# Top-k attention and two gated layers on one core: weights converted in place, differences one step behind

## The chip, the core and the metric

The kernel runs on one core of a Trainium2 chip. The time is the device time of one execution in microseconds (us); for the kernel before it is the median of three runs. The engines are named TensorE (PE in the rows, with its weight loads as PEld), VectorE (DVE), ScalarE (ACT), GpSimd (POOL) and SyncE (SP, which only issues DMAs here; SPq is its queue of them).

## The reference

Attention over 4 batches, 8 heads, 576 positions and a head size of 64, in which each query keeps its 32 largest scores; then two layers on 2304 tokens, each a product with a weight of 512 x 2048, a function of each element, and a product with a weight of 2048 x 512.

```python
scores = scale * np.matmul(q, k.transpose(0, 1, 3, 2))
kth = np.partition(scores, -top_k, axis=-1)[..., -top_k:-top_k + 1]
scores = np.where(scores >= kth, scores, -1e9)
attn = softmax(scores)
x = np.matmul(attn, v)                      # to (2304, 512)

h = x @ w_in                                # layer 1
P = a[0] + a[1] * h + a[2] * h**2 + a[3] * h**3
Q = 1.0 + abs(b[0]) * abs(h) + abs(b[1]) * h**2
x = (P / (Q + 1e-06)) @ w_out

h = x @ w_in2                               # layer 2
out = (h * cos(h)) @ w_out2
```

The four weights come as 64-bit floats. The chip has none, so the kernel takes each as two 32-bit words and makes of it a 32-bit float `a`, a rounded high part `h` (type fp32r, which TensorE takes in one pass) and a low part `a - h`. A product is then the sum of three: high by high, high by low and low by high.

## The kernel before

The work is cut into 72 units of attention (a query tile of 128 rows and a pair of heads). A unit consists of scores (`qk`, TensorE into `sx`, copied by ScalarE to `sS`), the selection of the 32 largest (`topk`: MAX8 and MATCH_REPLACE8 on VectorE over `e`, with two TENSOR_TENSOR ahead and, behind ScalarE's exponential, two SCALAR_TENSOR_TENSOR), and the product with v (`av`: transposes `pp`, copies `pt`). Layer 1 runs 9 units behind (`in1` to `out1`) and layer 2 18 units behind (`in2` to `out2`), in blocks of 256 tokens and 256 columns (`g`). Each unit is cut into five pieces, and the code is written in the order of pieces; a planner with its own estimate of time then lays each engine's instructions in order, up to a window of pieces. From unit 20 on (`U0`) the order is written out by hand (`unit`).

The conversions are 64 steps of 128 x 512 weights, `conv(kind, c, x)` at line 264: kind 0 is layer 1's input weight and kind 1 its output weight, in turns of four (`convs`, line 693), 32 in all; kinds 2 and 3 are those of layer 2, 16 and then 16. A conversion loads a raw tile of 128 x 512 x 2 words on SP, 512 KB (line 274). ScalarE turns the high word into a float in a buffer `cb` of its own (line 277) and the low word in place (line 278). Then VectorE shifts `cb` by three bits (TENSOR_SCALAR, line 281), GpSimd adds the low word (line 282), and ScalarE makes `h`. For kinds 0, 2 and 3 (`CPE`) the low part is taken by TensorE, which adds `a` by the identity and `h` by its negative into PSUM (`diff`), and a copy by ScalarE; for kind 1 GpSimd subtracts (line 299). SP stores the low part in HBM (`w1lo`, `w1ol`, `w2lo`, and `w2o`, which takes both parts of kind 3), and the layers stream it in later, through `lo`, `w1ol` and `w2o` (lines 490 to 498). High parts of kinds 0 to 2 stay on chip.

For layer 1's weights there are 5 raw tiles and 6 buffers `cb` (`RA`, `CA`), for layer 2's 3 and 4 (`RB`, `CB`), in a pool that is closed and opened again between them, since `w2hi` takes the place (line 268). At most three conversions are under way (`CD`), and none of layer 2 starts before layer 1's are through (`pull`, line 735). How far conversions have to be is tied to the pieces: the first 36 by piece 46, all by piece 80 (lines 972 to 975), and by what a product needs (`need`).

## Time and profile before

| | |
|---|---|
| Median of three runs | 1339.47 us (1338.54 to 1341.24) |
| The profiled execution | 1339.15 us, span 1337.4 us |
| Busy share of the span | TensorE 92%, VectorE 86%, ScalarE 82%, GpSimd 43% |
| Granted TensorE clock, mean | 0.971 |
| First and last load of a raw tile | 6.3 and 289.4 us |
| DMA | 314.98 MB, 236 GB/s |

Times in the rows are microseconds from the span's start, and ns where marked. Busy shares of the whole are means over stages that are limited by different engines, so the rows below are cut by stage: conversions of layer 1's weights (to 140 us), of layer 2's (to 310 us), and the stretch without conversions.

### The profile page before, as it was taken

What the parts mean: (1) busy time and instruction counts of PE and PEld (TensorE: products, weight loads), DVE (VectorE), ACT (ScalarE), POOL (GpSimd) and SP (SyncE); (2) the same over time, 40 slices, a digit from 0 to 9 for tenths busy, and PEclk for the clock granted to TensorE, in tenths of its full rate; (3) what the DMA queues carried; (4) which work ended last, traced back from release to release, by engine and by line L of the source; (5) the groups of instructions that cost most, each with busy time, mean ns of one, the idle gap of its engine ahead of it and who ended that gap; (6) DMA issues with size and microseconds to landing.
All of it is one profiled execution on the core that took longest, in us unless ns stands there. A gap on an engine that the chain in (4) does not pass through costs nothing.

```text
span 1337.4 us, 25132 instructions
## 1 busy us (share of the span) xinstructions
PE 1233.8 (92%) x8992; PEld 1086.7 (81%) x8992; DVE 1156.0 (86%) x2498; ACT 1093.7 (82%) x1871; POOL 569.6 (43%) x469
## 2 busy tenths in 40 slices
PE   6675678888999999999999999999999999999998
PEld 3343455656889999999989899999999999999996
DVE  6999879979799999999999999999999998755633
ACT  7887788886888898888898888888898888877753
POOL 2656444453245555445554444454444444430000
PEclk9676999999999999999999999999999999999999
DMA  8986777884356777667677776666677778877774
GB/s 254 335 278 223 247 239 246 275 311 132 122 190 217 231 245 248 215 218 229 208 234 239 246 230 210 213 217 200 217 234 265 268 283 288 297 235 235 235 258 155
DMA packets 155948, 314.98 MB, mean 236 GB/s; under 512 B 12592, under 2 KB 47536, under 8 KB 155824
## 3 DMA queue, kind: packets, MB, share of 16 engines
q1 hardware_dynamic: 122832, 261.99, 59.3%
q10 hardware_dynamic: 32992, 51.39, 12.0%
q8 instruction: 71, 1.16, 0.4%
q14 instruction: 53, 0.43, 0.1%
HBM read 278.20 MB, written 35.13 MB: 234 GB/s over the span
## 4 chain that ended last, share of the span: by engine, by line
PE 62%; DVE 13%; ACT 12%; DMA 4%; issue 4%; POOL 3%; ACTq 1%; SPq 0%; POOLq 0%; DVEq 0%
PE h L80 24%; PE o L80 12%; PE sx L80 10%; PE y L80 10%; DVE e L80 6%; DVE hd L80 3%; ACT r L80 2%; DVE u L80 2%; DMA raw<-w 1%; ACT sS L80 1%; ACT e L80 1%; ACT cb L80 1%; PE diff L80 1%; DVE cb L80 1%; ACT u L80 1%
## 5 line engine op out<-in xcount | busy, mean ns | idle before, releaser
L80 DVE MAX8 hd<-e 128x8 f32<-128x288 f32 (+1 forms) x576 | 320.9, 595 | 0.0
L80 POOL TENSOR_TENSOR gg<-rr,gg 128x512 fp32r<-128x512 f32 x56 | 72.3, 1292 | 400.8 <-DVE rr L80 185.4
L80 DVE MATCH_REPLACE8 e<-hd,e 128x288 f32<-128x288 f32 (+1 forms) x432 | 230.7, 539 | 0.0
L80 PE MATMUL o<-w2o,gg 128*128 128x512 f32 x864 | 223.6, 398 | 0.0
L80 PE MATMUL y<-gg,w1o 128*128 128x256 f32 x1152 | 216.1, 286 | 7.0 <-ACT gg L80 4.5
L80 PEld LDWEIGHTS y<-gg,w1o 128*128 128x128 f32 x1152 | 182.6, 193 | 12.5 <-ACT gg L80 7.1
L80 PEld LDWEIGHTS o<-w2o,gg 128*128 128x128 f32 x864 | 153.8, 189 | 27.0 <-DVE gg L80 0.3
L80 PE MATMUL h<-xh,w1hi 128*128 128x256 f32 x576 | 171.1, 297 | 4.7 <-ACT xh L80 3.2
L80 PE MATMUL h<-xl,w1hi 128*128 128x256 f32 x576 | 164.2, 285 | 2.5 <-DVE xl L80 2.5
L80 PE MATMUL y<-gg,w1ol 128*128 128x256 f32 x576 | 164.0, 285 | 0.0
L80 PE MATMUL h<-x2l,w2hi 128*128 128x256 f32 x576 | 163.0, 283 | 0.0
L80 PE MATMUL h<-xh,lo 128*128 128x256 f32 x576 | 162.8, 283 | 0.0
L80 PE MATMUL h<-x2h,lo 128*128 128x256 f32 x576 | 162.7, 283 | 0.0
L80 PE MATMUL h<-x2h,w2hi 128*128 128x256 f32 x576 | 162.7, 283 | 0.0
L80 DVE TENSOR_TENSOR e<-sS 128x576 f32<-128x576 f32 x144 | 118.2, 860 | 39.6 <-POOL q L80 27.9
L80 POOL TENSOR_TENSOR cb<-cb,raw 128x512 int32<-128x512 int32 x64 | 88.2, 1383 | 99.7 <-DVE cb L80 75.3
L80 DVE SCALAR_TENSOR_TENSOR e<-sS,hd,e 128x576 f32<-128x576 f32 x144 | 123.0, 882 | 5.9 <-ACT e L80 4.4
L80 PEld LDWEIGHTS h<-xh,w1hi 128*128 128x128 f32 x576 | 109.6, 190 | 17.2 <-issue 5.9
L80 PEld LDWEIGHTS h<-xl,w1hi 128*128 128x128 f32 x576 | 109.9, 191 | 7.7 <-DVE xl L80 4.4
L80 PEld LDWEIGHTS y<-gg,w1ol 128*128 128x128 f32 x576 | 111.4, 193 | 0.7 <-issue 0.4
L80 ACT ACTIVATE e<-sS,nb 128x576 f32<-128x576 f32 x144 | 105.6, 771 | 7.7 <-DVE hd L80 6.0
L80 PEld LDWEIGHTS h<-x2l,w2hi 128*128 128x128 f32 x576 | 110.2, 191 | 0.5 <-issue 0.2
(1026 smaller groups left out, 3272.5 us busy)
## 6 DMA issues: line engine op xcount, KB each, us to landing
w2o<-w2o SPq DMA_DIRECT2D x144, 512.0 KB, 4.2
lo<-w1lo SPq DMA_DIRECT2D x72, 512.0 KB, 3.9
w1ol<-w1ol SPq DMA_DIRECT2D x72, 512.0 KB, 4.8
lo<-w2lo SPq DMA_DIRECT2D x72, 512.0 KB, 4.6
k<-kdr ACTq DMA_DIRECT2D x44, 576.0 KB, 5.6
raw<-w SPq DMA_DIRECT2D x32, 512.0 KB, 5.7
v<-vt ACTq DMA_DIRECT2D x48, 320.0 KB, 4.2
qr<-qt ACTq DMA_DIRECT2D x72, 128.0 KB, 2.7
```

Source lines behind the costliest of these rows:

```text
L80: r = f(*a, **k)
```

## The change

- A conversion has no buffer `cb` any more. The float, the shift, the sum and `h`'s source lie in the raw tile, in every second word; the low part is then written over the tile's first half as a dense row.
- There are two pools of raw tiles, `near` (left) and `far` (right), of six tiles each. Layer 1's conversions take them in turn, layer 2's only `far`, and `w2hi` takes the place of `near`, as four tiles that wait for the old ones tile by tile. The wait for layer 1's conversions to be through is gone.
- A conversion has three steps: load and first two operations; shift, sum and `h`; difference and store. `step` puts the difference of conversion m - 1 behind the loads up to m + 5 (m + 4 for layer 2) and ahead of the shift of m.
- The difference goes over TensorE and ScalarE for all kinds.
- `w1lo`, `w2lo` and `w1ol` lie in HBM by pairs of column tiles, so a store has rows of 1 KB for 512 B, and a load rows of 4 KB for 2 KB.
- Kind 3's `h` takes the buffers of the attention's `q` tiles, which are unused before unit 22.

```diff
-RA, CA, RB, CB = 5, 6, 3, 4
+RL, RR = 6, 6
-CD = 3
+CD = 4
-CPE = (0, 2, 3)
...
+        near, far = temp("near", "left"), temp("far", "right")
...
         def conv(kind, c, x):
...
-            raw = tmps[0].tmp.tile([P, CW, 2], I32, tag="raw", bufs=n1, name="raw" + nm)
-            SP.dma_start(out=raw, in_=src)
-            a = tmps[0].tmp.tile([P, CW], F32, tag="cb", bufs=n2, name="cb" + nm)
-            lo, hi, ai = raw[:, :, 0], raw[:, :, 1], a.bitcast(I32)
-            A.activation(a, hi.bitcast(F32), AF.Prelu, scale=2.0 ** -112, alpha=-2.0 ** 32)
+            at, n = (near, RL) if i < n_w1 and i % 2 else (far, RR)
+            raw = at.tmp.tile([P, CW, 2], I32, tag="raw", bufs=n, name="raw" + nm)
+            SP.dma_start(out=raw, in_=wd.rearrange("(c p) (f t) -> c p f t", p=P, t=2)[c, :, x * CW:(x + 1) * CW, :])
+            lo, ai = raw[:, :, 0], raw[:, :, 1]
+            a = ai.bitcast(F32)
+            d = raw.rearrange("p f t -> p (f t)")[:, :CW].bitcast(F32)
+            A.activation(a, a, AF.Prelu, scale=2.0 ** -112, alpha=-2.0 ** 32)
             A.activation(lo, lo.bitcast(U32), AF.Copy, scale=2.0 ** -29)
+            yield
...
+            V.tensor_scalar(ai, ai, 3, 0, op0=ALU.logical_shift_left, op1=ALU.bitwise_or)
+            G.tensor_add(ai, ai, lo)
...
+            A.activation(h, a, AF.Copy)
+            yield
...
-                else:
-                    G.tensor_sub(a, a, h.bitcast(F32))
+            PE.matmul(o, ident, a, start=True, stop=False)
+            PE.matmul(o, nident, h, start=False, stop=True)
+            A.activation(d, o, AF.Copy)
...
+        def step(s, n):
+            while state[s] < n:
+                m = state[s]
+                if s == 0:
+                    state["cq"].append(conv(*convs[m]))
+                else:
+                    step(0, min(m + 1 + (CD if m < n_w1 else RR - 3), len(convs)))
+                    step(s - 1 if s == 2 else 2, m + 1 if s == 2 else m)
+                next(state["cq"][m], None)
+                state[s] += 1
```

Where this moves instructions is shown at three places. In these rows a conversion's tiles bear its c and x and a running number; `raw_0_0_290<-w` is kind 0 or 2, `<-w1o` kind 1, `<-w2o` kind 3, and `cb` is the buffer that is gone.

GpSimd, in the first conversions, before:

```order
L80 TENSOR_TENSOR cb_3_0_318<-cb_3_0_318,raw_3_0_316 128x512
L80 TENSOR_TENSOR cb_0_0_334<-cb_0_0_334,raw_0_0_332 128x512
L80 TENSOR_TENSOR cb_1_0_348<-cb_1_0_348,raw_1_0_346 128x512
L80 TENSOR_TENSOR cb_0_0_334<-cb_0_0_334,w1o 128x512
L80 TENSOR_TENSOR cb_2_0_365<-cb_2_0_365,raw_2_0_363 128x512
L80 TENSOR_TENSOR cb_1_0_348<-cb_1_0_348,w1o 128x512
```

And after:

```order
L79 TENSOR_TENSOR raw_3_0_302<-raw_3_0_302 128x512
L79 TENSOR_TENSOR raw_0_0_306<-raw_0_0_306 128x512
L79 TENSOR_TENSOR raw_1_0_319<-raw_1_0_319 128x512
L79 TENSOR_TENSOR raw_2_0_335<-raw_2_0_335 128x512
L79 TENSOR_TENSOR raw_3_0_348<-raw_3_0_348 128x512
```

The sums follow each other; the subtractions (`<-cb,w1o`) are gone from this engine.

TensorE, in units 0 to 2, before:

```order
L80 MATMUL diff<-cb_3_0_318,ident 128x512
L80 MATMUL diff<-w1hi,nident 128x512
L80 MATMUL sx<-kraw_1_146,qr_160 128x288 x4
L80 MATMUL pp1a<-ident,e_181 128x128 x4
L80 MATMUL pp1b<-ident,e_181 128x128 x4
```

And after:

```order
L79 MATMUL pp1a<-ident,e_184 128x128 x4
L79 MATMUL diff<-raw_3_0_302,ident 128x512
L79 MATMUL diff<-w1hi,nident 128x512
L79 MATMUL pp1b<-ident,e_184 128x128 x4
L79 MATMUL sx<-kraw_1_149,qr_163 128x288 x2
L79 MATMUL diff<-raw_0_0_306,ident 128x512
L79 MATMUL diff<-w1o,nident 128x512
```

The differences stand later among the transposes and scores, and those of kind 1 (`<-w1o,nident`) have come to them.

SP's queue, where layer 2's first differences are stored, before:

```order
L274 DMA raw_0_1_1131<-w 128x1024
L274 DMA raw_1_1_1195<-w 128x1024
L307 DMA w2lo<-cb_0_0_1090 128x4x128
L274 DMA raw_2_1_1258<-w 128x1024
L175 DMA kdr<-kraw_3_1156 64x576 x4
L307 DMA w2lo<-cb_1_0_1095 128x4x128
L274 DMA raw_3_1_1274<-w 128x1024
```

And somewhat later in the same stage, after:

```order
L309 DMA w2lo<-raw_0_1_1112 128x2x256
L273 DMA raw_2_2_1299<-w 128x1024
L309 DMA w2lo<-raw_1_1_1130 128x2x256
L273 DMA raw_3_2_1409<-w 128x1024
L487 DMA lo_0_4_1580<-w1lo 128x1024
L309 DMA w2lo<-raw_2_1_1193 128x2x256
L273 DMA raw_0_3_1430<-w 128x1024
```

Before, a load reuses a raw tile that GpSimd has read. After, `raw_2_2` reuses the tile of `raw_0_1`, which the store one row ahead of it reads, and so on: each load waits for the landing of the store of the sixth conversion before it.

## Rows read from the trace of the kernel before

**Rows 1.** Busy time by stretch: TensorE, weight loads, VectorE, ScalarE, GpSimd; clock, DMA share, GB/s.
```profile
20.00:140.00 120.00, 83.82 (x340) 49.14 (x339) 118.85 (x253) 95.51 (x185) 73.85 (x54) 0.77 0.84 272
140.00:300.00 160.00, 124.94 (x734) 92.85 (x734) 132.78 (x273) 134.23 (x256) 76.90 (x56) 0.96 0.81 267
345.00:1000.00 655.00, 645.73 (x5064) 595.94 (x5063) 615.04 (x1390) 576.19 (x971) 314.04 (x270) 1.00 0.68 219
```

**Rows 2.** First transposes of units 0, 8, 16: ns min/median/max, first and last start.
```profile
L80 PE MATMUL pp0a<-ident,e x4: 415/421/421, 29.1 to 29.7; 128*128 128x128 f32 x4
...
L80 PE MATMUL pp8a<-ident,e x4: 272/273/299, 137.3 to 137.6; 128*128 128x128 f32 x4
...
L80 PE MATMUL pp16a<-ident,e x4: 421/421/447, 300.4 to 301.0; 128*128 128x128 f32 x4
```

**Rows 3.** Waits of VectorE, 140 to 300 us: total us, times, longest.
```profile
DVE cb L80 <- ACT cb L80: 13.2, 6, 6.5
DVE u L80 <- POOL u L80: 6.5, 2, 4.3
```

**Rows 4.** VectorE's groups, 20 to 140 us: busy us, mean ns, idle before.
```profile
L80 DVE MAX8 hd<-e 128x8 f32<-128x576 f32 x33 | 23.6, 743 | 0.0
L80 DVE TENSOR_SCALAR cb<-cb 128x512 int32<-128x512 int32 x30 | 22.2, 746 | 0.0
L80 DVE SCALAR_TENSOR_TENSOR e<-sS,hd,e 128x576 f32<-128x576 f32 x18 | 20.2, 1125 | 0.2 <-ACT e L80 0.2
L80 DVE TENSOR_TENSOR e<-sS 128x576 f32<-128x576 f32 x18 | 19.2, 1100 | 1.1 <-PE sx L80 0.8 <-ACT sS L80 0.2
L80 DVE MAX8 hd<-e 128x8 f32<-128x288 f32 x34 | 14.0, 443 | 0.0
```

**Rows 5.** The same view, 320 to 400 us.
```profile
L80 DVE SCALAR_TENSOR_TENSOR e<-sS,hd,e 128x576 f32<-128x576 f32 x10 | 7.8, 812 | 1.7 <-ACT e L80 1.6
...
L80 DVE TENSOR_TENSOR e<-sS 128x576 f32<-128x576 f32 x10 | 7.1, 749 | 3.1 <-POOL q L80 3.1
```

**Rows 6.** The shift in the same view, 0 to 20 and 140 to 300 us.
```profile
L80 DVE TENSOR_SCALAR cb<-cb 128x512 int32<-128x512 int32 x2 | 0.8, 412 | 0.0
...
L80 DVE TENSOR_SCALAR cb<-cb 128x512 int32<-128x512 int32 x31 | 14.7, 477 | 13.2 <-ACT cb L80 13.2
```

**Rows 7.** GpSimd's subtractions, 20 to 140 us.
```profile
L80 POOL TENSOR_TENSOR cb<-cb,w1o 128x512 f32<-128x512 f32 x16 | 21.8, 1363 | 3.2 <-ACT w1o L80 3.2
```

**Rows 8.** ScalarE's groups of the conversions, 20 to 140 us.
```profile
L80 ACT ACTIVATE raw<-raw 128x512 int32<-128x512 uint32 x28 | 18.9, 674 | 2.6 <-DMA raw<-w1o 1.6 <-DMA raw<-w 1.0
...
L80 ACT ACTIVATE w1o<-cb 128x512 fp32r<-128x512 f32 x16 | 10.0, 627 | 1.1 <-POOL cb L80 1.1
...
L80 ACT ACTIVATE cb<-diff 128x512 f32<-128x512 f32 x16 | 9.4, 589 | 1.1 <-PE diff L80 0.9
```

**Rows 9.** The chain that ended last, 140 to 300 us, by engine and line.
```profile
by line: issue 12.5%; DVE e L80 10.4%; POOL cb L80 6.9%; DMA raw<-w 6.7%; DMA raw<-w2o 6.6%; DMA w2lo<-cb 6.5%; ACT cb L80 5.2%; DVE hd L80 3.5%; POOL q L80 3.1%; PE h L80 3.1%; PE diff L80 3.0%; ACT u L80 2.7%; ACT raw L80 2.6%; PE sx L80 
```

**Rows 10.** TensorE's timeline: one difference at full clock; start, us.
```profile
65.42 1.10 PE L80 MATMUL diff<-cb,ident 128*128 128x512 f32 x2 [1.46 <-ACT cb L80]
65.96 0.79 PE L80 MATMUL diff<-w1hi,nident 128*128 128x512 f32 x1
```

**Rows 11.** Stores of layer 2's differences, 140 to 300 us: KB, median us to landing.
```profile
w2lo<-cb SPq DMA_DIRECT2D x16, 256.0 KB, 3.9
...
w2o<-cb SPq DMA_DIRECT2D x13, 256.0 KB, 5.5
```

**Rows 12.** SP's timeline: layer 2's first load, first store, last load, last store.
```profile
138.07 1.28 SPq L274 DMA_DIRECT2D raw<-w  x3
...
155.37 0.38 SPq L307 DMA_DIRECT2D w2lo<-cb  x1
...
289.44 0.33 SPq L274 DMA_DIRECT2D raw<-w2o  x1
...
307.73 0.32 SPq L302 DMA_DIRECT2D w2o<-cb  x1
```

More of the change, by code (lines that the diff above doesn't have):

```diff
@@ L161, in load_k0 @@
         def load_k0(pr):
-            x = tmps[0].tmp.tile([P, 2, S], F32R, tag="kraw", bufs=RQ, name=f"kraw0_{pr}")
+            x = near.tmp.tile([P, 2, S], F32R, tag="kraw", bufs=RQ, name=f"kraw0_{pr}")
             SP.dma_start(out=x[:, 0].bitcast(F32), in_=kt[0, pr])
@@ L254, in body @@
         b0, b1 = babs[:, 0:1], babs[:, 1:2]
-        whi = [wts.tile([P, NCC, DF], F32R, name="w1hi")]
-        wlo = [dr.tile([NF, P, NCC, P], F32, name="w1lo"), dr.tile([NF, P, NCC, P], F32, name="w2lo")]
+        w1hi = wts.tile([P, NCC, DF], F32R, name="w1hi")
+        whi = [[w1hi[:, c] for c in range(NCC)]]
+        wlo = [dr.tile([NG, P, NCC, BT], F32, name="w1lo"), dr.tile([NG, P, NCC, BT], F32, name="w2lo")]
         w1o = wts.tile([P, NF, DM], F32R)
-        w1ol = dr.tile([NF, P, DM], F32)
+        w1ol = dr.tile([NG, P, 2, DM], F32)
@@ L260, in body @@
         w2o = dr.tile([NF, P, 2, DM], F32)
         late, diff = [], {}
+        convs = []
+        for x in range(4):
+            convs += [(0, c, x) for c in range(NCC)] + [(1, 4 * x + c, 0) for c in range(4)]
+        n_w1 = len(convs)
+        convs += [(2, c, x) for x in range(4) for c in range(NCC)] + [(3, c, 0) for c in range(NF)]
         def conv(kind, c, x):
             nm = f"{kind}_{c}_{x}"
-            wd = (w1_d, w1o_d, w2_d, w2o_d)[kind]
-            src = wd.bitcast(I32).rearrange("(c p) (f t) -> c p f t", p=P, t=2)[c, :, x * CW:(x + 1) * CW, :]
@@ new lines, in conv @@
+            A.activation(a, a, AF.Prelu, scale=2.0 ** -112, alpha=-2.0 ** 32)
+            A.activation(lo, lo.bitcast(U32), AF.Copy, scale=2.0 ** -29)
+            yield
+            if kind == 2 and len(whi) == 1:
+                near.close()
+                wts2 = pool("wts2", reuse_waits="tile")
+                whi.append([wts2.tile([P, DF], F32R, name=f"w2hi{j}") for j in range(NCC)])
+            V.tensor_scalar(ai, ai, 3, 0, op0=ALU.logical_shift_left, op1=ALU.bitwise_or)
+            G.tensor_add(ai, ai, lo)
@@ new lines, in conv @@
+            if kind == 3:
+                h = att.tile([P, 2, 2, P], F32R, tag="q", bufs=QB, name="ch" + nm).rearrange("p a b t -> p (a b t)")
+            elif kind == 1:
+                h = w1o[:, c, :]
+            else:
+                h = whi[kind // 2][c][:, x * CW:(x + 1) * CW]
+            A.activation(h, a, AF.Copy)
+            yield
+            if "d" not in diff:
+                diff["d"] = ps_o.tile([P, 2, 512], F32, tag="o", name="diff")
+            diff["n"] = n = diff.get("n", 0) + 1
@@ L691, in store @@
                 (SP if c == 0 else A).dma_start(out=out[row:row + n, :], in_=ob[c * n:(c + 1) * n, :])
-        convs = []
-        for x in range(4):
-            convs += [(0, c, x) for c in range(4)] + [(1, 4 * x + c, 0) for c in range(4)]
-        n_w1 = len(convs)
-        convs += [(2, c, x) for x in range(4) for c in range(4)] + [(3, c, 0) for c in range(NF)]
         need = {}
@@ L723, in body, with pull @@
                 loads.append((need.get(e, 0), load_w2o, e[1], e[2]))
-        state = {"conv": 0, "cq": [], "load": 0, "nl": 0}
-        def cstart():
-            if state["conv"] < len(convs):
-                state["cq"].append(conv(*convs[state["conv"]]))
-                state["conv"] += 1
-        def cfinish():
-            state["cq"].pop(0)()
-        def pull(n):
-            while state["conv"] - len(state["cq"]) < n:
-                while len(state["cq"]) < CD and state["conv"] < len(convs) and (state["conv"] != n_w1 or not state["cq"]):
-                    cstart()
-                cfinish()
+        state = {0: 0, 1: 0, 2: 0, "cq": [], "load": 0, "nl": 0}
+        def step(s, n):
[3 more added lines that the diff above has]
+                    state["cq"].append(conv(*convs[m]))
+                else:
+                    step(0, min(m + 1 + (CD if m < n_w1 else RR - 3), len(convs)))
+                    step(s - 1 if s == 2 else 2, m + 1 if s == 2 else m)
+                next(state["cq"][m], None)
+                state[s] += 1
+        def pull(n, last=2):
+            step(last, n)
         def run_event(e):
@@ L750, in run_event @@
             if e[0] is out1 and e[2] == NG - 1 and not late:
-                tmps.pop().close()
-                late.append(pool("late"))
+                far.close()
+                late.append(pool("late", side="right", reuse_waits="tile"))
             e[0](*e[1:])
```

65 lines of the change are left out of this document (21 added, 44 removed).

## The prediction

> **What bounds the kernel now.** I read the busy times by stretch first, because the change touches only work that lies in the first 310 us. From 345 to 1000 us TensorE is busy 645.73 of 655 us [rows 1]: nothing that the change does can shorten that stretch, and whatever the stretches before it gain or lose arrives at the end one to one. So the question is how fast units 0 to 19 run. I split them at 140 us, where the conversions of layer 1's weights end and those of layer 2's begin.
>
> From 20 to 140 us VectorE is busy 118.85 of 120 us [rows 1], so it stands idle for 1.15 us: it is the bound, at 108.2 us for eight units (29.1 to 137.3, [rows 2]). But its own work is not what fills the time. In this stretch the operations that read two tensors take 1100 and 1125 ns, and the shift on the weights 746 ns [rows 4]; where GpSimd has little to do the same forms take 749 and 812 [rows 5], and the shift takes 412 [rows 6]. The forms with one input at the slow rate (MAX8) take 743 ns in the busy stretch, so it is not VectorE that is slow: the others wait for a port that GpSimd holds. The excess is 18 x 0.351 + 18 x 0.313 + 30 x 0.334 = 6.3 + 5.6 + 10.0 = 21.9 us.
>
> From 140 to 300 us no engine is full: VectorE 132.78, ScalarE 134.23, TensorE 124.94 of 160 [rows 1], and the eight units take 163.1 us (137.3 to 300.4). VectorE's 27 us of idle time are led by 13.2 us for the shift's input (ScalarE's first step of a conversion) and 6.5 us for layer 1's product [rows 3]. The chain that ended last shows why those are late: loads of raw tiles hold 6.7 and 6.6% of it there and stores of layer 2's differences 6.5% [rows 9], 19.8% of 160, or 31.7 us. Raw tiles are loaded only when one of three is free, and a conversion starts only when one of four result buffers has been stored.
>
> **The change, part by part.**
>
> *Layer 1's output weights on TensorE.* GpSimd loses 16 subtractions of 1363 ns, 21.8 us [rows 7], all of them in the first stretch, out of its 73.85 us there: 29.5%. VectorE waits for GpSimd in proportion to the time that GpSimd holds the port, so I take 29.5% of 21.9 us: -6.5 us, and since VectorE is the bound there, all of it on the path. Bounds: nothing, if only the additions behind each shift collide, and -10 us, if the subtractions, which followed at once, made the queues of two.
> ScalarE gains 16 copies of 589 ns, 9.4 us [rows 8]. It goes from 95.5 to some 106 of 113.5 us, 94%: hidden, but barely; without that cover at worst the 9.4 us come back. TensorE gains 16 differences. One takes 1.33 us from the first start to the last end at full clock (65.42 to 66.75, [rows 10]), so 21 us; its 83.82 us hold stretches at the low clock (mean 0.77 of full, [rows 1]), so there is room, and I take nothing, at worst a few us of later qk and transposes.
>
> *In place.* The same instructions now step over 8 bytes. On ScalarE a rounding copy of dense data takes 627 ns and a copy that reads and writes at that step 674 [rows 8]: 64 x 0.047 = 3 us over the whole stage, hidden beside work that isn't full. On GpSimd one operand was strided already; no cost taken. On VectorE no strided shift is in the trace. It could stay at 412, or fall to the slow rate: MAX8 gives (743 - 443) / 288 = 1.04 ns an element, so 443 + 224 x 1.04 = 677 ns for 512. The first is nearer, since the shift alone runs at well under the slow rate and keeps dtype and size; and the loss would be small: MAX8 doesn't wait for GpSimd, so 677 would stand against 746 in the first stretch (-2 us), and against 477 for 31 shifts in the second (+6 us, [rows 6]). I take 0 and keep +4 for the range.
> The Trainium skill, "VectorE: DVE Perf Modes", section on mode 2x_2P, asks of the fast mode for 32-bit data only that source and destination lie in SBUF and that their outermost dimension be even, not that the step be one. By it the term is 0, by the other end +4; no run here shows a strided shift yet.
>
> *Twelve raw tiles, then six, and the difference one step behind.* In the first stretch VectorE waits for nothing, so loads that come sooner gain nothing there. At the change of layer the old pools had to drain; now loads for layer 2 stand among the last stores of layer 1. In the second stretch a raw tile is held from its load to the landing of its difference: six tiles do what three raw and four result buffers did. The loads run four conversions ahead instead of two. I count against this what the new order puts on SP: a load of conversion m + 6 stands one to three rows behind the store of m and waits for its landing, and everything on SP, layer 1's streamed weights too, is queued behind it. A cycle of SP is then landing plus issues: 3.9 us for layer 2's input weights, 5.5 for its output weights [rows 11], each with 0.4 us for every DMA in between. Without overlap 16 x 5.0 + 10 x 6.9 = 149 us for the 26 loads that wait, 5.7 each. But two pairs of stores stand together before their two loads, and others have another store or a stream between, so I take off some 13 us: 136 us, 5.2 each. Before, 32 conversions took 138.1 to 307.7 us, 5.3 each.
> From the first store of layer 2 (155.4 before [rows 12]; I take 146, as its loads no longer wait for the drain) the last load then goes out at 146 + 136 = 282 us, where it was 289.4: 7 us sooner. From the other side: the two waits that a late raw tile explains are 13.2 us and the longest of the 6.5 us, 4.3: 17.5 us, and half of it would be 9. The two meet, and I take **-9 us**; bounds -20 (all such waits and half of the rest) and +5 (5.7 us a cycle: the last load at 294).
>
> *The rest.* Layer 2's input weights in four tiles, the wider rows of the two low parts in HBM, the pools that wait by tile: the same transfers and matmuls, under TensorE at 99% after 345 us. DMA engines are 68% busy there [rows 1]. Nothing.
>
> **The sum**: -6.5 + 0 - 9 = -15.5 us, rounded to -15. The span of 1337.4 becomes 1322.4; 1.75 us lie around it in the profiled execution (1339.15), which makes 1324.2, and the median stood 0.3 above that execution: **1324.5 us**.
>
> **The rivals.**
> *ScalarE takes VectorE's place* in the first stretch (94% by the sum, in order, with waits of its own): the -6.5 are lost and only the second stretch gains: 1331. For it: the margin; against: VectorE's work is far ahead in its queue, and it was idle for 1.15 us.
> *The stalls go altogether*: VectorE keeps only its waits for scores and half of the rest, -20, and -9 in the first stretch: 1310. Against: every load of the second half waits for a landing.
> *Slower: SP's queue is the new bound.* At 5.7 us a cycle the last load leaves at 294, 5 us late, and a difference that is one step behind adds a cycle, 5.7, before the last store: +10.7, less 6.5: 1343.5. It decides from 5.3 us a cycle on, the pace before; the landings of [rows 11] lie on both sides of that. Against it: landings were measured with loads in the queue ahead of them, and a queue that waits has fewer of these. The Trainium skill, "DMA: Bandwidth & Descriptors", section on the anatomy of one DMA, says that semaphore waits are held by the issuing sequencer before dispatch; this rival is that rule at work on SP.
> *The change doesn't do what it says*: the planner lays the loads as late as before, or the shift falls to the slow rate and the copies crowd ScalarE. Gains and losses cancel: within 3 us of 1339.
>
> **How the numbers follow.** Forecast (1316 to 1330) 0.52; ScalarE as bound, or another half gain (1330 to 1336) 0.15; stalls gone (below 1316) 0.11; cancelled (within 0.2%, 2.7 us, about what a measurement can tell from no change) 0.09; slower 0.13. Faster 0.78, same 0.09, slower 0.13. For eight in ten the range goes down to 1308, which holds nearly all of the larger gain, and up to 1340, which leaves out the slower case: 1308 to 1340.
>
> **What would show it.** Unit 16's first transpose (300.4) should come near 285 us, and unit 8's (137.3) near 131. VectorE's two-input forms before 140 us should fall by about a tenth, and the shift to 640 ns or so there with 412 where GpSimd is idle; a floor of 677 would show the slow rate. VectorE's wait for the shift's input should fall from 13.2 to some 5 us. If SP is the bound, its queue shows loads waiting for landings of differences at 5.3 us a conversion or more, and ScalarE waits for raw tiles as before. If ScalarE is the bound, VectorE waits for scores or exponentials before 140 us. The forecast is wrong if units 0 to 7 are no faster, or if TensorE is no longer full from 345 us on.

## The result and the profile after

The change made the kernel slower: 1355.31 us (median of five runs, 1351.39 to 1358.78) beside 1338.71 for before on the same chip (median of five, 1337.22 to 1341.24). The ratio on record is 1.0108 with an interval of 1.0091 to 1.0126; the two medians alone give 1.0124. The prediction said 1324.5 us, faster, with 1308 to 1340 us as the range for eight in ten.

The profiled execution of after took 1358.78 us, the longest of the five; its span is 1357.0 us, before's was 1337.4. The 19.6 us between them are some 3 us more than the medians differ by. Every kernel below has one profile, and its runs spread over 4 to 14 us, so a difference of a few us between two profiles is no finding. Where the 19.6 us came is read from the first transposes of units 0, 8 and 16, as in [rows 2]. TensorE's timeline of after; start us, us:

```profile
26.05 1.11 PE L79 MATMUL pp0a<-ident,e 128*128 128x128 f32 x4
...
155.35 0.66 PE L79 MATMUL pp8a<-ident,e 128*128 128x128 f32 x4
...
318.37 0.66 PE L79 MATMUL pp16a<-ident,e 128*128 128x128 f32 x4
```

Unit 8 comes 18 us later than before (137.3), although unit 0 comes 3 us sooner. Units 8 to 16 take 163.0 us, as before (163.1). From unit 16 to the end it is 1038.6 us beside 1037.0. So the loss lies in the first stretch and the gain of the second did not come. In the first stretch it lies between units 2 and 8: unit 2 still starts at 50.1 us, where it was 56.7.

Busy time by stretch in after, columns as in [rows 1]:

```profile
20.00:140.00 120.00, 92.19 (x333) 50.71 (x331) 96.42 (x227) 97.64 (x188) 44.96 (x38) 0.80 0.78 254
140.00:300.00 160.00, 128.67 (x676) 93.65 (x676) 118.10 (x267) 122.61 (x234) 61.00 (x49) 0.88 0.74 235
345.00:1000.00 655.00, 642.38 (x5054) 592.08 (x5055) 617.31 (x1393) 573.11 (x967) 314.81 (x269) 1.00 0.68 216
```

VectorE, which had stood idle for 1.15 of 120 us before [rows 1], is now idle for 23.6. GpSimd fell from 73.85 to 44.96 us. VectorE's groups from 20 to 140 us in after, the answer to [rows 4] (busy us, mean ns, idle before), and behind them the shift over the whole span (ns min/median/max):

```profile
L79 DVE MAX8 hd<-e 128x8 f32<-128x576 f32 x29 | 20.8, 744 | 0.0
L79 DVE SCALAR_TENSOR_TENSOR e<-sS,hd,e 128x576 f32<-128x576 f32 x16 | 16.1, 1015 | 6.7 <-ACT e L79 6.7
L79 DVE TENSOR_SCALAR raw<-raw 128x512 int32<-128x512 int32 x32 | 15.9, 498 | 6.0 <-ACT raw L79 5.8 <-issue 0.2
L79 DVE TENSOR_TENSOR e<-sS 128x576 f32<-128x576 f32 x15 | 13.6, 947 | 10.9 <-PE sx L79 10.9
```
```profile
L79 DVE TENSOR_SCALAR raw<-raw x64: 382/426/1635, 15.8 to 315.1; 128x512 int32<-128x512 int32 x64
```

Two things are to be seen. The excess over the free durations of [rows 5, 6] is now 16 x 0.203 + 15 x 0.198 + 32 x 0.086 = 9.0 us, where it was 21.9: the forms that the prediction has waiting for GpSimd's port became faster, by twice the 6.5 us that it took. (The runs e1 and e5 below show that the subtractions alone do not set this size.) And all of it, and more, went into the right-hand column: VectorE waits for a buffer `e` (the rows' `PE sx`, explained below), for exponentials and for weights. MAX8 is unchanged, as it was to be.

SP's queue shows loads (line 273) that wait for the landing of the difference that last lay in their tile. In before, loads of raw tiles waited for GpSimd to have read the tile (24.3 us from 20 to 140 us, 40.2 from 140 to 300), and hardly ever for a landing. Waits of SP's queue in after, 20 to 140 us and then 140 to 300 us (total us, times, longest):

```profile
SPq L273 <- DMA w1lo<-raw: 26.5, 12, 4.5
...
SPq L273 <- DMA w1ol<-raw: 16.2, 7, 4.1
...
SPq L273 <- DMA w2lo<-raw: 53.3, 15, 7.4
SPq L273 <- DMA w2o<-raw: 20.7, 8, 5.1
```

The chain that ended last has the same in a piece from 113 to 123 us of after (start us, us, what): a landing, then the load that waited for it, then ScalarE, which waited for the load.

```profile
113.30 4.87 DMA w1lo<-raw
118.20 0.03 issue
118.23 3.92 DMA raw<-w1o
...
122.25 0.68 ACT raw L79
```

And so it reaches VectorE. The timeline of after from 84 to 106 us (start us, us, then the instruction, its idle time ahead of it and what ended that):

```profile
84.82 1.11 PE L79 MATMUL pp4a<-ident,e 128*128 128x128 f32 x4
...
97.71 1.21 ACT L79 ACTIVATE raw<-raw 128x512 f32<-128x512 f32 x2 [1.93 <-DMA raw<-w]
98.82 0.64 ACT L79 ACTIVATE sS<-sx 128x576 f32<-128x576 f32 x1
...
99.51 2.29 PE L79 MATMUL sx<-kraw,qr 64*128 64x288 f32 x4 [2.67 <-ACT sS L79]
101.72 2.08 PE L79 MATMUL diff<-raw,ident 128*128 128x512 f32 x2
...
104.87 0.42 PE L79 MATMUL sx<-ident,e 128*128 128x128 f32 x1
...
105.33 0.76 DVE L79 TENSOR_TENSOR e<-sS 128x576 f32<-128x576 f32 x1 [2.57 <-PE sx L79]
```

ScalarE, in order, stands still for 1.93 us until a raw tile has landed. Behind it in its queue is the copy of scores that frees `sx`, so TensorE waits 2.67 us. Behind TensorE's scores stands a difference, and behind that the last transposition of unit 4, `sx<-ident,e` at 104.87, 20.1 us after the first of that unit (84.82). VectorE waits 2.57 us for this one: its next work is unit 6's, there are two buffers `e`, and unit 4's has to be read out first.

So `PE sx` in these rows is not a wait for scores. All five such waits of after in the first stretch (10.9 us) end with a unit's last transposition, and hold back the unit two later. In units 1 to 7 it comes 13.6 to 20.1 us behind the unit's first in after, 4.0 to 11.7 us in before, and 5.5 to 9.8 us in e17, the fastest run below, where this wait does not occur.

The life of a raw tile shows why loads meet landings. Matching the load, rounding, difference and store of each conversion in the order in which the program lays them, the means for conversions 12 to 31 in after are: load 4.8 us, 0.8 to ScalarE's first step, 10.4 to the rounding, **28.8 from the rounding to its difference**, 5.8 to the landing: 50.6 us. Before, the time from rounding to difference was 4.1 us. On ScalarE's queue a difference stands behind the roundings of five to nine later conversions in most of layer 1, not of one. Twelve tiles at 50.6 us are 4.2 us a conversion; the loads of conversions 12 to 31 went out every 4.6 us (30.5 to 118.2), where it was 3.8 before (43.2 to 115.5).

### The profile page after: what moved, and what is told of

Read it like the earlier page. It is cut to its first block, busy times and chain, and to the rows that moved or that the text cites. A ratio compares the mean times of both kernels' runs of the same rounds, so it can differ in the third digit from the quotient of the medians.

```text
span 1357.0 us, 25291 instructions
## 1 busy us (share of the span) xinstructions
PE 1261.6 (93%) x9040; PEld 1098.0 (81%) x9040; DVE 1133.6 (84%) x2498; ACT 1102.3 (81%) x1887; POOL 535.3 (39%) x453
## 4 chain that ended last, share of the span: by engine, by line
PE 42%; ACT 19%; DVE 18%; DMA 12%; issue 4%; POOL 3%; ACTq 2%; SPq 1%; POOLq 0%; DVEq 0%
PE h L79 13%; PE o L79 9%; PE y L79 8%; PE sx L79 7%; DVE e L79 6%; DVE hd L79 5%; ACT r L79 3%; ACT sS L79 3%; DMA raw<-w 3%; ACT raw L79 3%; DVE u L79 2%; DMA w2lo<-raw 2%; DVE rr L79 2%; PE diff L79 2%; DMA raw<-w2o 2%
## 5 line engine op out<-in xcount | busy, mean ns | idle before, releaser
L79 PE MATMUL y<-gg,w1ol 128*128 128x256 f32 x576 | 163.7, 284 | 0.0
L79 DVE TENSOR_TENSOR e<-sS 128x576 f32<-128x576 f32 x144 | 109.0, 797 | 46.4 <-POOL q L79 24.6
L79 POOL TENSOR_TENSOR raw<-raw 128x512 int32<-128x512 int32 x64 | 71.6, 1121 | 153.0 <-ACT raw L79 87.2
L79 ACT ACTIVATE raw<-raw 128x512 f32<-128x512 f32 (+1 forms) x128 | 79.6, 675 | 55.2 <-DMA raw<-w 31.8
L79 PE MATMUL diff<-raw,ident 128*128 128x512 f32 x128 | 88.5, 778 | 31.0 <-ACT raw L79 20.0
```

The costliest lines, as they stand in the source:

```text
L79: r = f(*a, **k)
```

## The experiments

Theories. **A**, crowding: sixteen more differences make TensorE and ScalarE the bound. **B**, tile life: a raw tile is held until its difference has landed. **C**, order: the difference is late because the code writes it one step behind. **D** came up with the first runs: twelve tiles are too many for the first stretch. The table gives the ratio to before on the same chip with its interval, the start of unit 8, the time of units 8 to 16, the mean time from rounding to difference in conversions 12 to 31 (those on GpSimd included), and the last landing of layer 1, all in us from the profiled executions.

| run | ratio | unit 8 | 8 to 16 | to difference | last landing |
|---|---|---|---|---|---|
| before | 1 | 137.3 | 163.1 | 4.1 | 138.0 |
| after | 1.0108 (1.0091 to 1.0126) | 155.3 | 163.0 | 28.8 | 162.0 |
| e1_cpe | 1.0031 (1.0013 to 1.0048) | 143.9 | 163.8 | 10.8 | 150.0 |
| e2_k1pool | 1.0017 (0.9997 to 1.0037) | 149.8 | 156.1 | 4.5 | 136.6 |
| e3_hstore | 1.0016 (0.9998 to 1.0034) | 145.3 | 156.6 | | |
| e4_eight | 1.0188 (1.0137 to 1.0239) | 138.9 | 186.0 | 11.2 | 155.5 |
| e5_two_six | 1.0074 (1.0045 to 1.0104) | 138.3 | 171.6 | 11.1 | 157.3 |
| e6_two_six_pool | 0.9958 (0.9932 to 0.9985) | 137.9 | 159.1 | 2.3 | 138.5 |
| e7_old_buffers | 1.0085 (1.0058 to 1.0111) | 152.8 | 163.1 | 3.5 | 142.6 |
| e8_not_behind | 1.0134 (1.0092 to 1.0175) | 156.7 | 167.5 | 27.2 | 166.4 |
| e9_lag3 | 1.0047 (1.0029 to 1.0064) | 146.5 | 157.8 | 10.8 | 153.4 |
| e10_lag2_all | 1.0014 (0.9989 to 1.0040) | 141.4 | 163.7 | 6.8 | 151.3 |
| e11_pool_lag2 | 0.9975 (0.9955 to 0.9996) | 137.4 | 161.0 | 2.2 | 136.9 |
| e12_pool_lag1 | 0.9988 (0.9968 to 1.0008) | 138.1 | 162.0 | 2.3 | 138.7 |
| e13_l2_hstore | 0.9941 (0.9923 to 0.9960) | 138.5 | 149.9 | | |
| e14_small_diff | 0.9941 (0.9923 to 0.9959) | 145.7 | 152.6 | 3.3 | 148.2 |
| e15_near_early | 0.9964 (0.9947 to 0.9982) | 141.7 | 157.2 | 3.0 | 142.0 |
| e16_both | 0.9937 (0.9919 to 0.9956) | 142.8 | 154.0 | | |
| e17_both_nine | 0.9909 (0.9889 to 0.9928) | 133.9 | 153.3 | | |

### One part of the change alone, or undone

In the kernel before:
```diff
-CPE = (0, 2, 3)
+CPE = (0, 1, 2, 3)
```

> The kernel before with one part of the change alone: layer 1's output weights take their difference on TensorE and ScalarE too; raw tiles, result buffers and order of steps stay as they were. Theory A (crowding: sixteen more differences make TensorE and ScalarE, which work in order and wait for each other, the bound of the first stretch): all or most of the loss comes back, 1350 to 1357 us, with unit 8's first transpose at 145 us or later. Theory B (tile life: a raw tile is now held until its difference has landed in HBM, and ScalarE stands in front of late loads): this kernel has separate result buffers and gains what the prediction said, 1331 to 1336 us, unit 8 near 131. Theory C (order: the difference one step behind): as B.

Neither. 0.3% slower: the differences alone, with the old buffers, cost 4 us where the prediction had -6.5, and are less than a third of the loss. Unit 8 is 6.6 us late. VectorE's three forms from 20 to 140 us in e1 (busy us, mean ns, idle before):

```profile
L80 DVE TENSOR_TENSOR e<-sS 128x576 f32<-128x576 f32 x16 | 18.3, 1184 | 6.1 <-PE sx L80 6.1
L80 DVE TENSOR_SCALAR cb<-cb 128x512 int32<-128x512 int32 x30 | 18.0, 602 | 2.1 <-ACT cb L80 2.1
L80 DVE SCALAR_TENSOR_TENSOR e<-sS,hd,e 128x576 f32<-128x576 f32 x16 | 17.6, 1104 | 0.1
```

The excess is 16 x 0.435 + 30 x 0.190 + 16 x 0.292 = 17.3 us, 4.6 less than before, and VectorE, busy for 111.66 us, is idle for 8.3. So already here the relief comes, somewhat under 6.5 us, and the waits take more than it gives.

In the kernel after:
```diff
+            if kind == 1:
+                G.tensor_sub(d, a, h.bitcast(F32))
+            else:
+                ...
```

> The kernel after with that one part undone: layer 1's output weights take their difference on GpSimd again, from the strided tile into its dense first half, with twelve tiles and the step behind as they are. Theory A (crowding): the first stretch runs as before or better, unit 8 at 137 us or sooner, 1330 to 1339 us. Theory B (tile life): nearly all of the loss stays, 1350 to 1357 us, since tiles are still held to the landing. Theory C (order): as B.

The total fits neither theory fully (1343.59 us): most of the loss is gone, but unit 8 still comes at 149.8, far from A's 137. The time from rounding to difference fell from 28.8 to 4.5 us with this one edit, which B as I had put it did not see: fewer differences on TensorE, a shorter queue of them, a shorter tile life.

```diff
-                SP.dma_start(out=w1ol[c // 2, :, c % 2, :], in_=d)
+                SP.dma_start(out=w1ol[c // 2, :, c % 2, :], in_=h.bitcast(F32))
```
(and the other low parts likewise)

> The kernel after with the stores of the low parts reading the rounded weights (w1hi, w1o, w2hi, ch) in place of the difference: same bytes, same descriptors, but no raw tile waits for a landing any more, and SP's stores don't wait for the difference. The low parts in HBM are therefore the rounded weights, and the products that use them come out otherwise. Theory B (tile life, the part that is landing): the 42 us for which SP waits for landings before its loads in 50 to 155 us go, ScalarE's 15 us of waits for raw tiles shrink to a third, unit 8 comes at 140 us or sooner, 1333 to 1342 us. Theory A (crowding): the differences are still there, 1350 to 1357 us. Theory C (order): 1350 to 1357 us.

1343.96 us, just above B's range: with the landing taken out of a tile's life and all differences still on TensorE, most of the loss is gone, against A and C. (The run takes out a second thing with it: SP's stores no longer wait for the differences, 20.8 us in after from 20 to 140 us.) Both stretches gain (145.3, 156.6). But unit 8 is 8 us later than before, so landings are not all of it.

```diff
-RL, RR = 6, 6
+RL, RR = 4, 4
```

> The kernel after with eight raw tiles in place of twelve, four in each pool (so layer 2 has four in place of six). In the order laid down a difference then stands 3 or 4 conversions behind its rounding in place of 7 to 9. Theory B (tile life): with a third fewer tiles and the same life the first stretch takes longer still, 10 us or more above after, 1365 to 1380 us. Theory A (crowding): tiles are not what runs short, the queue in front of the differences only becomes shorter: 1350 to 1358 us. If twelve tiles themselves are the harm (conversions laid far ahead of the scores that VectorE needs): 1338 to 1348 us.

The total is in B's range, but by the wrong stretch. With a third **fewer** tiles the first stretch is 16 us shorter than in after (unit 8 at 138.9), and layer 2, with four tiles for six, is 23 us longer. That is the third case for layer 1 and B for layer 2.

### Eight tiles for layer 1, six for layer 2

```diff
-RL, RR = 6, 6
+RL, RR = 2, 6
-        at, n = (near, RL) if i < n_w1 and i % 2 else (far, RR)
+        at, n = (near, RL) if i < n_w1 and i % 4 == 0 else (far, RR)
```

> The kernel after with eight raw tiles for layer 1 (two in one pool, six in the other, dealt one to three) and six for layer 2 as in after. With four and four, unit 8 came at 138.9 us (after: 155.3), and only layer 2, with four tiles, lost (units 8 to 16 took 186 us, after: 163). Theory D (twelve tiles are too many for the first stretch: they let the differences fall 7 to 9 conversions behind, and TensorE, ScalarE and SP, each in order, then wait for one another): unit 8 at 137 to 142 us, units 8 to 16 in 156 to 163, 1334 to 1343 us. Theory B (tile life, more tiles are better everywhere): unit 8 later than in after, 1358 us or more.

Unit 8 as D says (138.3), the total not (1353.82): units 8 to 16 take 171.6. Layer 1's last difference lands at 157.3 us, 19 us after unit 8 began. Layer 2's tiles are loaded from 129.2 us on, but their differences stand behind layer 1's: the first comes at 159.4 us, in e6 at 141.1.

The same, with e2's edit:

> The same with two and six raw tiles, and layer 1's output weights taking their difference on GpSimd again. Theory D: both crowding effects are gone; VectorE's two-input forms wait for GpSimd's port again, so unit 8 comes where it was before the change, 133 to 139 us, and units 8 to 16 take the 156 us that they took in the run with GpSimd's differences and twelve tiles: 1327 to 1337 us. If the shorter difference alone was what that run gained by (theory A), the number of tiles adds nothing: 1341 to 1346 us.

As D said: 1336.65 us, faster than before. Of e5 and e6, VectorE's three forms and its stretch, 26 to 138 us, with layer 1's output weights on TensorE (e5) and on GpSimd (e6); busy us, mean ns, idle before, and then the windows with the columns of [rows 1]:

```profile
L79 DVE SCALAR_TENSOR_TENSOR e<-sS,hd,e 128x576 f32<-128x576 f32 x16 | 16.0, 1014 | 1.6 <-ACT e L79 1.6
L79 DVE TENSOR_SCALAR raw<-raw 128x512 int32<-128x512 int32 x30 | 15.5, 520 | 6.6 <-ACT raw L79 3.7 <-issue 2.9
L79 DVE TENSOR_TENSOR e<-sS 128x576 f32<-128x576 f32 x14 | 11.8, 883 | 3.5 <-PE sx L79 3.5
```
```profile
L79 DVE TENSOR_SCALAR raw<-raw 128x512 int32<-128x512 int32 x30 | 20.1, 674 | 0.0
L79 DVE SCALAR_TENSOR_TENSOR e<-sS,hd,e 128x576 f32<-128x576 f32 x16 | 17.8, 1115 | 0.0
L79 DVE TENSOR_TENSOR e<-sS 128x576 f32<-128x576 f32 x16 | 17.4, 1123 | 0.9 <-PE sx L79 0.9
```
```profile
26.00:138.00 112.00, 85.79 (x349) 48.93 (x347) 99.59 (x236) 95.46 (x185) 39.53 (x35) 0.91 0.83 268
```
```profile
26.00:138.00 112.00, 83.89 (x328) 47.84 (x328) 111.10 (x240) 92.23 (x178) 65.71 (x51) 0.78 0.86 293
```

This is the clearest pair of the study. Against [rows 5, 6] the excess is 8.3 us in e5 and 18.7 in e6, 10.4 less; the idle time is 12.4 and 0.9 us, 11.5 more. Unit 8 starts at 138.3 and 137.9. What VectorE no longer loses in slow forms it loses in waits for TensorE and ScalarE, although none of the three is full in e5: VectorE is busy for 99.59, ScalarE for 95.46 and TensorE for 85.79 of 112 us.

Layer 1 with raw tiles and `cb` as before, layer 2 as in after:
```diff
+            if i < n_w1:
+                d = a = near.tmp.tile([P, CW], F32, tag="cb", bufs=6, name="cb" + nm)
+                A.activation(a, ai.bitcast(F32), AF.Prelu, ...)
+                ai = a.bitcast(I32)
```

> Layer 1 with the buffers of before (raw tiles and six dense result buffers, difference of the output weights on GpSimd), layer 2 in place in six raw tiles as after; steps one behind in both. Theory D: the first stretch as before (unit 8 at 135 to 139 us), the second 156 to 163: 1329 to 1339 us. If the change of layer 2 is itself worth nothing (units 8 to 16 took 163.1 us before and after): 1338 to 1342 us.

Missed: 1354.04 us, and the first stretch is what went wrong. VectorE in e7, 26 to 153 us:

```profile
L79 DVE SCALAR_TENSOR_TENSOR e<-sS,hd,e 128x576 f32<-128x576 f32 x18 | 24.7, 1380 | 0.6 <-ACT e L79 0.5
...
L79 DVE TENSOR_TENSOR e<-sS 128x576 f32<-128x576 f32 x14 | 17.2, 1264 | 2.4 <-PE sx L79 2.4
```

With the buffers of before, and one raw tile more, the two forms that took 1125 and 1100 ns before [rows 4] take 1380 and 1264, although GpSimd is busy for as large a share as before (77.32 of 127 us; before 73.85 of 120). So what they lose beside GpSimd is not set by its busy share alone; what sets it these rows don't show. A comparison of layer 2 by this run is then not clean; units 8 to 16 take 163.1 us in it.

### Order and lag

```diff
             A.activation(h, a, AF.Copy)
-            yield
             if "d" not in diff:
```

> The kernel after with the difference written directly behind the rounding in place of one step behind; all else as in after. In the order that the planner lays down from it the differences stand as far behind as in after (7 to 9 conversions in layer 1). Theory C (the step behind delays the differences): unit 8 at 145 us or sooner, 1335 to 1345 us. Theories A, B and D: what the program writes one step behind decides nothing, 1350 to 1358 us.

C falls: 1361.16 us, 27.2 us from rounding to difference. Where the code writes the difference does not decide where this planner lays it.

The lag can be bounded by a rule of order on ScalarE:
```diff
-            A.activation(h, a, AF.Copy)
+            hc = A.activation(h, a, AF.Copy)
+            far_d = diff.get(i - (3 if i < n_w1 else 9))
+            if far_d:
+                tc.add_manual_dep(hc.ins, far_d, ORDER, reason="lag")
...
-            A.activation(d, o, AF.Copy)
+            diff[i] = A.activation(d, o, AF.Copy).ins.name
```

> The kernel after, twelve tiles and all, with one more rule of order on ScalarE for layer 1: the rounding of conversion m stands behind the copy of the difference of m - 3, so a difference stands at most three roundings behind its own (after: 7 to 9). Theory D in its sharper form (ring): a load waits for a landing, the landing for a difference, the difference for the rounding that stands ahead of it, so only twelve less eight tiles move freely, one cycle of load, conversion and store (4.8 + 0.6 + 10.6 + 5.8 = 21.8 us) for four conversions, 5.4 us each; with nine free tiles it is 2.4 and the ring no longer bounds. Then unit 8 comes at 136 to 145 us and units 8 to 16 take 163 as in after: 1336 to 1346 us. If it is the number of tiles as such, or the sixteen differences, and not the lag: 1350 us or more.

Half: 1349.11 us, unit 8 at 146.5, just outside. The time to the difference fell from 28.8 to 10.8 us, but the time from ScalarE's first step to the rounding rose from 10.4 to 20.2, so a tile's life only fell from 50.6 to 44.2. So a shorter lag alone gives half of what eight tiles give at unit 8.

> The kernel after with the same rule for both layers and a bound of two. Ring: layer 1 as with three; layer 2 has six tiles and a lag of 3 to 4 for its input weights in after, where a conversion took 6.6 us (before: 4.7); with a lag of 2 four tiles move freely in place of two or three, 5.4 us or less each, so units 8 to 16 take 150 to 158 us in place of 163: 1326 to 1340 us. If the lag is not what bounds layer 2: as with the bound of three in layer 1 alone, within 4 us.

1343.74 us, above the range. First stretch better again (141.4), the second not (163.7): missed there. The tiles of layer 2's input weights live 37.6 us as in after (37.4); the waiting moved from behind the rounding to ahead of it.

Two runs with the rule on layer 2 alone, in e6:

> The kernel with two and six raw tiles and layer 1's output weights on GpSimd (1336.7 us, units 8 to 16 in 159.1), with the rule of order for layer 2 alone, bound two (there without it: 3 to 4 roundings for the input weights). The first stretch is laid down as it was. Ring: a conversion of layer 2's input weights takes 4.5 us in place of 5.0, units 8 to 16 take 148 to 156: 1326 to 1334 us. If the lag doesn't bound layer 2: 1334 to 1340 us.

> The same with a bound of one: the rounding of conversion m stands behind the difference of the one before, as the code writes it. Ring: five of six tiles move freely, as fast as or faster than with two, 1324 to 1334 us. If ScalarE's order becomes too tight (each rounding now waits for TensorE's difference of the one before, and all that stands behind it on ScalarE too): 1340 us or more, with ScalarE waiting for TensorE's difference by 10 us or more in units 8 to 16.

161.0 and 162.0 us for units 8 to 16, the totals 1340.11 and 1340.40 (0.9975 and 0.9988 of before, e6 0.9958): no gain over e6. The other reading of e12 is not what happened either: ScalarE waits for TensorE's difference by 0.2 us in units 8 to 16, not by 10. For layer 2's input weights the time from rounding to difference fell from 13.7 us in e6 to 5.0 in e12, and the time to the rounding rose from 6.5 to 16.3. In layer 2 the lag is not the bound.

### What bounds the second stretch

All three start from e6.
```diff
-                SP.dma_start(out=w2o[c, :, 1, :], in_=d)
+                SP.dma_start(out=w2o[c, :, 1, :], in_=h.bitcast(F32))
```
(and `w2lo` likewise)

> The kernel with two and six raw tiles and layer 1's output weights on GpSimd (1336.7 us, units 8 to 16 in 159.1), with layer 2's stores of low parts reading the rounded weights in place of the difference: same bytes, but no raw tile of layer 2 waits for a landing. Layer 2's low parts in HBM are therefore the rounded weights, and its products come out otherwise. If tile life sets layer 2's pace: each of the six tiles is free 5 us sooner of some 32, a conversion takes 4.5 us in place of 5.2, units 8 to 16 take 147 to 153 us, 1325 to 1331 us. If something else sets it (VectorE, ScalarE and TensorE waiting for one another with the work of the units): 157 to 162 us for units 8 to 16 and 1334 to 1339 us.

149.9 us for units 8 to 16, as tile life says. Like e3 it takes out two things, the landing from a tile's life and the stores' wait for the difference; e14 separates them. The total, 1334.07, gained less than the range: units 16 to 20 then take 74 us (e6: 70). SP's waits from 140 to 300 us in e6, and then in e13:

```profile
SPq L273 <- DMA w2lo<-raw: 36.2, 14, 6.2
...
SPq L273 <- DMA w2o<-raw: 15.4, 7, 4.7
```
```profile
SPq L273 <- ACT raw L79: 39.2, 18, 5.4
```

The loads no longer wait for landings, and ScalarE's waits for raw tiles fell from 17.2 to 8.8 us.

```diff
+                if i >= n_w1:
+                    d = far.tmp.tile([P, CW], F32, tag="dt", bufs=2, name="dt" + nm)
                 A.activation(d, o, AF.Copy)
-RL, RR = 2, 6
+RL, RR = 2, 5
```

> The same base with layer 2's differences written into two tiles of their own of 2 KB, in place of the sixth raw tile of 4 KB: five raw tiles, each free when TensorE has read it, and two differences that wait for landings. If tile life sets layer 2's pace: five tiles of some 26 us, 5.2 us a conversion, the same as six of 32: 1334 to 1340 us. If the landing on SP's queue is what costs (a load stands behind the landing of its own tile): 1328 to 1334 us.

1335.08 us, at the border of the two, though the stretches tell: units 8 to 16 in 152.6 with five tiles, 6.5 us less than with six; layer 1, with seven tiles, is 7.8 us later. Here the stores still wait for the differences (33.8 and 23.1 us from 150 to 300 us) but the loads now wait for TensorE to have read a tile (27.7 us) and no longer for layer 2's landings, so it is the landing ahead of a load that costs, for the most part. In the second stretch two small tiles beside five are better than a sixth; by their totals e14 and e6 can't be told apart.

```diff
-        at, n = (near, RL) if i < n_w1 and i % 4 == 0 else (far, RR)
+        at, n = (near, RL) if i < 20 and i % 4 == 0 else (far, RR)
```

> The same base, but the near pool's two tiles are dealt only to conversions before the 20th, so that the place for layer 2's input weights comes free some 30 us sooner (last landing from it near 100 us in place of 118); the six far tiles carry the rest. If that handover holds up layer 2's start: unit 10 sooner by 3 to 8 us, 1328 to 1334 us. If not (in this base the rounding of layer 2's first weights waits for nothing longer than 5 us): the same within 3 us, or slower by the two tiles that the last twelve conversions of layer 1 lack.

1337.34 us, and no gain at the handover: units 8 to 10 take 32.4 us, in e6 28.3, and unit 10 comes at 174.1 us, in e6 at 166.2.

### Both findings together

Five far tiles and two small ones, with three near tiles (dealt three in eight) in e16 and four (every second conversion) in e17.

> The kernel with five far raw tiles and two small tiles for layer 2's differences, and three near tiles in place of two (dealt three in eight), so that layer 1 has eight raw tiles again; layer 1's output weights on GpSimd. With two and five, unit 8 came at 145.7 us and units 8 to 16 took 152.6; with two and six 137.9 and 159.1. If the two findings add up: unit 8 at 137 to 140 us, units 8 to 16 in 150 to 155: 1326 to 1332 us. If what the first stretch gains is lost again in the second: 1333 to 1338 us.

> The same with four near tiles, dealt every second conversion: nine raw tiles for layer 1. By the finding that differences on GpSimd keep the lag at 1 to 4 whatever the number of tiles, the ninth tile changes little: unit 8 at 136 to 142 us, 1326 to 1334 us. If more tiles than eight already do harm: unit 8 at 143 us or later, 1334 us or more.

e16 is at 1333.77 us, the second stretch as if both added up (154.0) and the first not (142.8), though layer 1 has eight tiles as in e6 (137.9). e17 is the fastest of all, 1327.92 us, 0.9909 of before. Its unit 8 is sooner than expected: the ninth tile, which was to change little, brings it 8.9 us forward. TensorE's timeline of e17, and its busy times from 20 to 140 us with the columns of [rows 1]:

```profile
133.94 0.90 PE L79 MATMUL pp8a<-ident,e 128*128 128x128 f32 x3
...
287.25 0.60 PE L79 MATMUL pp16a<-ident,e 128*128 128x128 f32 x4
```
```profile
20.00:140.00 120.00, 94.39 (x362) 55.69 (x360) 120.00 (x270) 103.03 (x200) 74.58 (x58) 0.76 0.86 290
```

Both stretches are shorter than before, by 3.4 and 9.8 us; at the end of the profiled execution 8.7 us are left (span 1328.7). VectorE is full again, 120.00 of 120 us, beside a GpSimd that is as busy as before. e17 keeps the change's conversion in place, gives layer 1 nine tiles in place of twelve, leaves its output weights on GpSimd, and frees layer 2's tiles before the landing.

## Why the prediction was wrong, point by point

- **What bounds the kernel.** Right for before: VectorE full from 20 to 140 us, TensorE after 345. That the later stages hand a loss on one to one held in after: 18.0 us at unit 8, 18.0 at unit 16, 19.6 at the end. Over all runs it holds less well: from unit 16 to the end they take 1034.5 to 1043.9 us, before 1037.0.
- **The differences on TensorE, -6.5 us.** This is the step that failed: "since VectorE is the bound there, all of it on the path". In none of the three pairs that differ in it alone was it a gain. Ratios to before:

  | tiles for layer 1 | differences of the output weights on TensorE | on GpSimd |
  |---|---|---|
  | twelve | 1.0108 (after) | 1.0017 (e2) |
  | eight | 1.0074 (e5) | 0.9958 (e6) |
  | buffers of before | 1.0031 (e1) | 1 (before) |

  The edit costs 0.9%, 1.2% and 0.3%, some 12, 16 and 4 us. The relief itself was there: the excess fell by 12.9 us in after, by 10.4 in e5 against e6 and by 4.6 in e1 against before. (That it goes in proportion to GpSimd's time, as I took it, e7 contradicts.) But VectorE's idle time grew by 22.4, 11.5 and 7.2 us. VectorE was full, and the orders of TensorE and ScalarE stood right behind it. That is near the first rival (ScalarE takes VectorE's place), to which I gave too little, but not as I had written it: ScalarE is busy for 97.64 of 120 us in after, 81% and not 94%, and of VectorE's waits before 140 us the exponentials are 6.7 us, while the 10.9 us at `PE sx` are a late transposition that holds a buffer, and not scores. Beyond it I missed that layer 1's last differences come later: they have landed at 157.3 us in e5 and at 138.5 in e6, and layer 2's stand behind them.
- **In place, 0 us.** Right for the instructions; no run has this part alone. The strided shift has a median of 426 ns and a minimum of 382, beside 412 [rows 6]; the slow rate would be 677. The Trainium skill, "VectorE: DVE Perf Modes", section on mode 2x_2P, asks for no step of one; the trace agrees with it. ScalarE's rounding copies rose from 627 [rows 8] to 689 ns, 0.06 us where I took 0.047.
- **Twelve tiles in the first stretch, 0 us.** A term that I put at nothing with half a reason: I wrote that loads which come sooner gain nothing there, and took it that they lose nothing either. Differences fell five to nine roundings behind, a tile lived 50.6 us, and ScalarE stood before late tiles. At unit 8 this lost most: eight tiles (e4, e5) bring it from 155.3 to 138.9 or 138.3, no landings (e3) to 145.3, a bounded lag (e9) to 146.5, GpSimd's differences (e2) to 149.8. In the total it lost less: by the table above some 8 us with the differences on GpSimd, and with them on TensorE some 5, which is within the intervals, since there (e5) the second stretch takes 171.6 us. Both parts undone (e6) give back some 20 us, more than the loss. "One step behind" I read as one conversion of time; e8 shows that the text of the code decides nothing about it here.
- **Six tiles in the second stretch, -9 us.** It came to 0 in after, to -4 in e6. The gain that I took for the missing drain came: layer 2's first rounding stands 5.6 us behind the start of unit 8 (160.9 and 155.3), where it was 11.6 (148.9 and 137.3). The pace did not: from the first rounding of layer 2 to the last it takes 163.4 us, before 156.6. The reckoning of SP's cycle was the right place to look, and the slower rival described what is seen: loads wait for landings. The Trainium skill, "DMA: Bandwidth & Descriptors", section on the anatomy of one DMA, has waits held by the issuing sequencer; the 53.3 and 20.7 us of SP's waits are that. VectorE's wait for the shift's input, which was to fall from 13.2 us to some 5, rose to 24.1, and ScalarE's waits for raw tiles from 10.7 to 32.9. What I mis-sized is the tile's life: I counted landing and issue, some 6 us, but the tile is held from its load to the landing, 37.4 us for the input weights and 30.9 for the output weights, so that six tiles give one conversion in 6.2 and 5.2 us. (That is an account and no cause: e12 took some 9 us out of one part of the life and they came back in another. And the first of these tiles were loaded from 122.8 us on and then lay until layer 1's last differences had been taken.) That the landing ahead of a load costs is shown by e13 and e14: from the first rounding to the last 152.5 and 147.2 us, in e6 161.6. My -9 was there to be had, e17 has it (-9.8), but not with six tiles that wait for their landings.
- **The rest, 0 us.** No run has these parts alone. From unit 16 on, after is within 1.6 us of before.
- **The rivals.** The slower one gave 1343.5 us, from SP in the second stretch with the gain of the first kept. The loss was another: 18 us in the stretch where the worst that I had priced was the 9.4 us of ScalarE's copies and a few us on TensorE.

What stays open is how the 17 us between units 8 of e5 and after divide between lag, landings and the mere number of tiles, since each changes the order that the planner lays. The number alone does not decide: with the differences on GpSimd unit 8 comes at 145.7 us with seven tiles (e14), at 137.9 and 142.8 with eight (e6, e16), at 133.9 with nine (e17) and at 149.8 with twelve (e2). Open is also why the two-input forms are so slow in e7.

## What to carry to other kernels

A full engine is a bound only until it is relieved: before counting a relief, ask what the engines right behind it would then make it wait for. More buffers can be slower where the order on each queue is fixed by a planner: here, with twelve tiles, it laid more work ahead of the step that frees a buffer, and with the differences on GpSimd unit 8 came soonest with nine. Count a buffer's whole life, step by step, divide by the number of buffers, and compare the pace with the one needed; then test what holds it, since a part of the life that is shortened can come back in another. Read in the rows which instruction ended a wait, and not only the name of its tile. A buffer that is read by a store lives through its landing, so a small buffer for what is stored can be worth more than another large one.

## What the runs showed that I had not expected

From 26 to 138 us TensorE's mean granted clock, a mix of its two levels (1.2 and 2.4 GHz), was 0.91 in e5 and 0.78 in e6, where the sixteen differences are on GpSimd. TensorE was busy for 85.79 and 83.89 us there, only 2 us apart, although I had reckoned the differences at 21 us. Its differences take 44.90 us in e5 and 32.11 in e6, and all else 40.89 and 51.78 (262 and 281 instructions). A product with the identity, of which a difference has two, has a median of 617 ns in e5 and of 1055 in e6. The total did not gain by it: 1353.82 and 1336.65 us. From 20 to 140 us the clock was 0.77 in before, 0.89 in e1 and 0.80 in after, with TensorE busy for 83.82, 93.07 and 92.19 us; which of the changes moves it no run isolates.

GpSimd's addition took longer into a dense buffer than in place: 1401 ns before, 1444 in e1 and 1388 in e7 on `cb` (20 to 150 us), 1139 in after, 1071 in e5 and 1151 in e6 in the strided tile, where e6 has the subtractions of before beside it. I had taken no difference.
